# New queue orders for four engines of a transformer block on one Trainium2 core

## Chip, cores and metric

The kernel runs on one core of a Trainium2 chip. The metric is the time of one execution in microseconds (us); the median of several runs is given. The core has a matrix engine (TensorE, in the profile PE, with its weight loads as PEld), a vector engine (VectorE, DVE), an activation engine (ScalarE, ACT), a general engine (GpSimd, POOL) and a queue that only issues transfers here (SyncE, SP). Each engine works off its own queue of instructions strictly in order; what crosses engines is held by semaphores.

## What is computed

One block over 2048 rows of 448 values, in bf16: a layer norm, linear attention with 16 heads of 28 features and a softmax feature map, a residual, a second layer norm, a gated feed-forward of width 1792, and a second residual.

```python
qkv = norm(x) @ wqkv                        # q, k, v: 16 heads, 28 features each
pq, pk = q @ w_phi, k @ w_phi               # per head
phi_q = concat([softmax(pq), softmax(-pq)]) # over the features of a head
phi_k = concat([softmax(pk), softmax(-pk)])
kv = einsum("bhsf,bhsd->bhfd", phi_k, v);  z = phi_k.sum(over s)
o = (phi_q @ kv) / (phi_q @ z + 1e-6)
h = x + o @ wo
g, u = norm(h) @ w_gate, norm(h) @ w_up
out = h + (sigmoid(g) * u) @ w_down
```

## The kernel before

The rows lie in 16 tiles of 128, numbered 0 to 15; four tiles make a chunk of 512. A class Graph takes every step as a named operation with its reads and writes, and derives from the program's order who must wait for whom. The order in which an engine works off its steps is another thing: it is written out by hand in the table ORDER, one string of names per engine. A step that may run on more than one engine (given as a tuple of engines) runs on the one whose string has its name. So a change of the strings moves steps in a queue or between engines, and touches neither the work nor the dependences. No planner runs when the kernel is built.

The names, in the order of the work, with the number of the tile behind them and the line of the profile in brackets:

- Start: warm (L478) are matmuls on zeros; zero, bd0, v1ones, phipad, opad0, mask0 to mask2, ident0, ident, neghalf and wqpad fill constants. x1, x0, x2, ... load tiles of x (x2 loads tiles 2 and 3, and so on); ld_k, ld_v, ld_q, wphi load attention weights.
- Layer norm 1: bst and agg (L499, L500) are the statistics, ve1, pow1, nm1, nb1 (L507, L512, L510, L516) make the reciprocal deviation and the shift, xn (L525 on ScalarE, L528 on VectorE or GpSimd) the normalised tile. The rstd steps serve groups: tiles 0, 1, 2, 3, then 4-5, 6-7, 8-11, 12-15, named by the first. xT turns the tile over: tiles 0 to 3 by a matmul (L492) and a copy xTe (L485), the others by a transfer that SyncE issues (L538).
- Weights folded with w_phi: wT (L554), its copy wTe, w2m (L567), its copy w2e (both copies L485); w2m0, w2e0 for k, w2m1, w2e1 for q.
- Projections of k and v (L296): ppa, ppb and vva, vvb for tiles 0 to 3 in pairs, pva, pvb for one tile from 4 on. An "a" and a "b" step are the two halves of one accumulation on the array's two row halves, and b waits for a. Then v1 copies v out (L485), ek takes both exponentials (L614, L615), ss and rs the softmax sums and reciprocals (L618, L619), phi the product (L622), and kva, kvb (L296) add phi times v into two banks that kvzA to kvzD (L683, L687) copy out at the end; kvzones sets their ones. Three buffers hold phi, five each ek and v1.
- Attention per chunk and tile: pqa, pqb (L296) and eq (L652, L653) for q; num (L296), and behind it rsm, qq, b, c, den, rden on VectorE (L714 to L725), o (L729), oT (two by L492, the others by SyncE, L742), woa, wob (L296) and h (L748 on ScalarE, L751 on VectorE). num of all tiles from 2 on writes the same two banks, so it waits for the den before it.
- Layer norm 2: nm, sq, ve, pow2, hn (L754, L756, L759, L761, L765), hT (two by L492, the others by SyncE, L772).
- Feed-forward: ga, gb (L296) with gate and up, sig (L824), hh (L825), dn, dp, dm, dl (L296, L852) with w_down, fin (L859), out. ga0_1 is the second feature block of tiles 0 and 1; ga2, ga4, ga8 and ga12 are the later groups of tiles.

An evacuation may run on ScalarE or VectorE, xn on up to three engines, phi and o on GpSimd or VectorE:

```python
op(("act", "dve"), name, (lambda e: e.copy(dst, src), lambda e: e.tensor_copy(dst, src)), r=[rkey], w=[wkey])
op(("act", "dve", "pool"), "xn%d" % t, (fa, fd, fd), r=r + [("nb1", a)], w=[("xn", s)])
op(("pool", "dve"), "phi%d" % t, fphi, r=[("ek", s), ("rs", s)], w=[("phi", sp)])
```

## Time and profile before

| | |
|---|---|
| median of 3 runs | 205.54 us (205.32 to 205.71) |
| span of the profiled execution | 203.7 us, 5834 instructions |
| time of the profiled execution outside its span | not listed; the median of the runs is 1.8 us over the span |
| busy share of the span | PE 97%, PEld 55%, DVE 67%, ACT 48%, POOL 28% |
| TensorE clock granted | 1.00 of full speed in every stretch |

The span runs from the first to the last instruction of the program. Busy times are in us. The chain that ended last is followed back from the last instruction: at each step to what released it, or to the instruction before it on its engine. A line of a timeline has the start in us from the span's start, the time in us, the engine, the line of the kernel, the operation, what it writes and reads, how many were merged, and in brackets the idle time of the engine before it and who ended it. A tile view gives durations as least, median and most.

### The profile page before, as it was taken

To read this page: it belongs to the slowest core of one execution; us is meant where nothing else is said; L and a number is where in the kernel's file an instruction comes from. 1 tells how busy PE (TensorE), PEld (TensorE's weight loads), DVE (VectorE), ACT (ScalarE), POOL (GpSimd) and SP (SyncE) were. 2 spreads that over 40 slices of the span, in tenths; PEclk is the share of its full clock that TensorE was granted. 3 is DMA by queue.
4 is the path that set the end of the run, shared out by engine and by line. 5 is a ranking of instruction groups with operands and counts; after the bars stand their busy time and mean duration, and the time that the engine had idled before them with its cause. 6 is when DMAs were issued, how large, how long until landed. Compare 5 with 4: busy or idle time off the path is not lost.

```text
span 203.7 us, 5834 instructions
## 1 busy us (share of the span) xinstructions
PE 196.7 (97%) x2474; PEld 111.6 (55%) x2474; DVE 135.9 (67%) x340; ACT 97.4 (48%) x195; POOL 57.9 (28%) x98
## 2 busy tenths in 40 slices
...
GB/s 163 306 139 122 77 73 66 282 295 352 141 52 55 55 100 27 55 81 0 3 0 80 119 30 28 2 77 24 56 36 60 3 0 3 0 0 138 0 0 90
DMA packets 32866, 16.25 MB, mean 80 GB/s; under 512 B 25096, under 2 KB 31944, under 8 KB 32840
## 3 DMA queue, kind: packets, MB, share of 16 engines
...
q8 instruction: 19, 0.31, 0.7%
q10 hardware_dynamic: 504, 0.03, 0.2%
...
## 4 chain that ended last, share of the span: by engine, by line
PE 89%; DVE 4%; ACT 3%; DMA 1%; issue 1%; POOL 0%; DVEq 0%
PE psum L296 82%; PE psum L852 5%; DVE st L499 2%; DMA x_sb<-in_A_x_dram 1%; ACT eq L653 1%; ACT eq L652 1%; PE psum L567 1%; ACT junk L756 1%; ACT x_sb L748 1%; PE psum L492 1%; DVE kvz L683 1%; DVE mv L500 0%; DVE b_sb L717 0%; DVE c_sb L720 0%; POOL rst L512 0%
## 5 line engine op out<-in xcount | busy, mean ns | idle before, releaser
L296 PE MATMUL psum<-xnT,wg_sb 64*128 64x512 bf16 (+1 forms) x490 | 93.3, 333 | 0.4 <-ACT eq L653 0.2
L296 PE MATMUL psum<-xnT,wu_sb 64*128 64x512 bf16 (+1 forms) x490 | 93.0, 333 | 0.0
L824 ACT ACTIVATE sg_sb<-psum 128x512 bf16<-128x512 f32 (+1 forms) x70 | 35.0, 512 | 89.6 <-PE psum L296 89.0
L825 DVE SCALAR_TENSOR_TENSOR hhT<-sg_sb,psum 128x512 bf16<-128x512 bf16 (+1 forms) x70 | 39.0, 577 | 52.5 <-ACT sg_sb L824 52.1
L296 PEld LDWEIGHTS psum<-xnT,wg_sb 64*128 64x128 bf16 x490 | 44.3, 94 | 22.9 <-DVE hhT L825 4.8
L296 PEld LDWEIGHTS psum<-xnT,wu_sb 64*128 64x128 bf16 x490 | 44.3, 94 | 13.0
L296 PE MATMUL psum<-wd_sb,hhT 64*128 64x448 bf16 x336 | 36.9, 349 | 0.0
L296 PEld LDWEIGHTS psum<-wd_sb,hhT 64*128 64x128 bf16 x336 | 17.3, 94 | 14.8 <-DVE x_sb L751 0.6
L622 POOL TENSOR_TENSOR phi<-hhT,rs 128x896 bf16<-128x896 bf16 x14 | 24.1, 1738 | 0.9 <-PE psum L296 0.8
L296 PE MATMUL psum<-Wk,xnT 64*128 64x448 bf16 x112 | 22.3, 350 | 0.2
L296 PE MATMUL psum<-wv_sb,xnT 64*128 64x448 bf16 x112 | 22.4, 351 | 0.1
L759 POOL TENSOR_SCALAR ve<-ssq 128x1 f32<-128x1 f32 x16 | 3.1, 192 | 66.1 <-ACT junk L756 65.7
L618 DVE TENSOR_REDUCE ss<-hhT 128x32 f32<-128x896 bf16 x16 | 17.0, 1062 | 0.7 <-ACT hhT L615 0.7
L296 PE MATMUL psum<-xnT,Wq 64*120 64x512 bf16 x112 | 15.0, 385 | 0.1
L729 POOL TENSOR_TENSOR o_pad<-c_sb,rden 128x448 bf16<-128x448 bf16 x10 | 9.3, 936 | 15.6 <-DVE rden L725 13.4
L296 PE MATMUL psum<-wo_o,oT 64*128 64x448 bf16 x56 | 13.2, 350 | 0.0
L296 PE MATMUL psum<-wo_e,oT 64*128 64x448 bf16 x56 | 13.1, 349 | 0.0
L756 ACT ACTIVATE junk<-x_sb,nm 128x448 bf16<-128x448 bf16 x16 | 10.6, 661 | 1.9 <-DVE nm L754 1.8
L852 PE MATMUL psum<-wd_sb,hhT 128*128 128x448 bf16 (+2 forms) x70 | 11.1, 316 | 0.0
L859 DVE SCALAR_TENSOR_TENSOR x_sb<-psum,x_sb 128x448 bf16<-128x448 f32 (+2 forms) x17 | 9.4, 591 | 2.1 <-PE psum L852 1.6
L499 DVE BATCH_NORM_STATS2 st<-x_sb 128x6 f32<-128x448 bf16 x16 | 9.4, 611 | 1.9 <-DMA x_sb<-in_A_x_dram 1.9
L296 PEld LDWEIGHTS psum<-Wk,xnT 64*128 64x128 bf16 x112 | 7.6, 94 | 5.3 <-ACT hhT L615 0.7
...
## 6 DMA issues: line engine op xcount, KB each, us to landing
...
```

The lines of the kernel that those rows point to most:

```text
L296: p = e.matmul(o, lhsT=w, rhs=r, start=st, stop=sp, tile_position=(row, 0))
L492: p = e.transpose(ps[:, kt * P:(kt + 1) * P], src, ident[:])
L499: op("dve", "bst%d" % t, lambda e: e.bn_stats(st1[:, t, :], x_sb[:, t, :]), r=[("x", t)], w=[("st1", t)])
L618: op("dve", "ss%d" % t, lambda e: e.tensor_reduce(ss[:, s, :], eks, AX.X, ALU.add), r=[("ek", s)], w=[("ss", s)])
L622: return e.tensor_tensor(phi[:, sp, :, :, :].rearrange("p b a n -> p (b a) n")[:, :, 0:56].rearrange("p b (h d) -> p b h d", h=2), eks.rea ...
L729: return e.tensor_tensor(o_pad[:, t % NO, off:off + D].rearrange("p (h d) -> p h d", h=H), c_sb[:, t % NS, :, 0:DH], rden[:, t % NS, :][:, ...
L756: op("act", "sq%d" % t, lambda e: e.activation(junk[:, t % 2, :], h_sb[:, t, :], ACT.Square, bias=nm2[:, t:t + 1], accum_out=ssq2[:, t:t + ...
L759: op("pool", "ve%d" % t, lambda e: e.tensor_scalar(ve2[:, t:t + 1], ssq2[:, t:t + 1], 1.0 / D, EPS, op0=ALU.mult, op1=ALU.add), r=[("ssq2" ...
L824: op("act", "sig" + nm, lambda e: e.activation(sg_sb[:, k, 0:N], bk(bg)[:, 0:N], ACT.Tanh, scale=0.5), r=[B(bg)], w=[("sg", k)])
L825: op("dve", "hh" + nm, lambda e: e.scalar_tensor_tensor(out=hhT[(t0 // 4) % NHH][:, ff, ns], in0=sg_sb[:, k, 0:N], scalar=1.0, in1=bk(bu)[ ...
L852: p = e.matmul(bk(b)[:, lo:hi], lhsT=hb[:, ff, TS(t)], rhs=wd_sb[:, ff, lo:hi], start=ff == 0, stop=ff == FT - 1)
L859: op("dve", "fin%d%s" % (t, nm), lambda e: e.scalar_tensor_tensor(out=h_sb[:, t, lo:hi], in0=bk(b)[:, lo:hi], scalar=0.5, in1=h_sb[:, t, l ...
```

## The change

The strings of ScalarE, TensorE, VectorE and GpSimd are computed anew up to about the first groups of gate and up; behind them they are as they were, and SyncE's has the same names in the same order (its lines are only wrapped in another place). Some steps also change the engine:

- from ScalarE to VectorE: wTe0, wTe2, xT1e, kvzones; from ScalarE to GpSimd: xn4
- from VectorE to GpSimd: xn0, xn1, nm1_0, nm1_6, nm1_8, ve1_1, ve1_12, phi10, o8
- from GpSimd to VectorE: nm1_1, nm1_2, nm1_3, nm1_4, nm1_12, ve1_0, ve1_2, ve1_3, ve1_6, phi11, o2, o7

TensorE keeps all its steps. No operation, load, buffer or dependence is added or removed.

```diff
     "act": (
-        "wphi3 wphi2 wphi1 wphi0 wTe0 wTe1 xT1e xT0e wTe2 w2e0_0 w2e0_1 w2e0_2 w2e0_3 xn3 xn4 ek0 ek1 xn5 v1_0 v1_1 "
-        "xn6 ek2 v1_2 v1_3 ek3 w2e1_1 ek4 v1_4 ek5 v1_5 w2e1_0 v1_6 ek6 xn11 ek7 v1_7 xn12 ek8 xn13 ek9 w2e1_3 w2e1_2 "
-        "ek10 xn14 ek11 xn15 v1_11 ek12 eq0_0 ek13 v1_13 ek14 v1_14 ek15 kvzones v1_15 eq0_1 kvzB eq1_0 eq1_1 eq2_0 "
-        "oT0e eq2_1 h1 h0 sq1 sq0 eq3_0 eq3_1 sig0_1 sig0_0 sig0_3 sig0_2 sig0_5 sig0_4 sq2 sig0_7 sig0_6 sq3 sig0_9 "
-        "sig0_8 sq5 sig0_11 sig0_10 sig0_13 sig0_12 sig2_1 sig2_0 sq4 sig2_3 sig2_2 sq7 sq6 sig2_5 sig2_4 sig2_6 "
...
+        "wphi3 wphi1 wphi2 wphi0 wTe1 w2e0_0 w2e0_2 w2e0_1 w2e0_3 xT0e xn3 ek0 ek1 xn5 v1_1 v1_0 xn6 ek2 v1_2 v1_3 "
+        "ek3 w2e1_1 ek4 v1_4 w2e1_0 ek5 v1_5 ek6 v1_6 xn11 ek7 v1_7 xn12 ek8 xn13 ek9 w2e1_2 w2e1_3 ek10 xn14 xn15 "
+        "ek11 v1_11 ek12 eq0_0 ek13 v1_13 ek14 ek15 v1_14 v1_15 eq0_1 kvzB eq1_0 eq1_1 eq2_0 oT0e eq2_1 h1 h0 sq1 "
+        "sq0 eq3_0 eq3_1 sig0_1 sig0_0 sig0_3 sig0_2 sig0_5 sig0_4 sig0_7 sig0_6 sq3 sq2 sig0_9 sig0_8 sig0_11 "
+        "sig0_10 sig0_13 sig0_12 sig2_1 sig2_0 sq4 sq5 sig2_3 sig2_2 sq7 sq6 sig2_5 sig2_4 sig2_6 sig2_7 sig2_8 "
...
     "pe": (
-        "warm0 warm1 warm2 wT0 wT1 xT1 warm3 xT0 warm4 warm5 wT2 w2m0_0 wT3 warm6 w2m0_1 w2m0_2 warm7 w2m0_3 warm8 "
-        "ppa0 warm9 ppb0 vva0 xT3 xT2 vvb0 ppa2 ppb2 vva2 vvb2 w2m1_1 w2m1_0 kva0 pva4 kvb0 pvb4 pva5 kva1 pvb5 kvb1 "
-        "pva6 kva2 pvb6 pva7 w2m1_2 w2m1_3 pvb7 pva8 kvb2 kva3 pvb8 kvb3 pva9 kva4 pvb9 kvb4 pva10 kva5 pvb10 pva11 "
-        "kvb5 kva6 pvb11 pqa0_0 pva12 kvb6 kva7 pvb12 kvb7 pqb0_0 kva8 pva13 kvb8 kva9 pvb13 pva14 kvb9 kva10 pvb14 "
-        "kvb10 kva11 pva15 kvb11 pvb15 kva12 pqa0_1 kvb12 pqb0_1 kva13 pqa1_0 kvb13 kva14 pqb1_0 kvb14 kva15 kvb15 "
-        "pqa1_1 num0 num1 pqb1_1 pqa2_0 pqb2_0 num2 pqa2_1 oT0 pqb2_1 oT1 num3 woa0 wob0 num4 pqa3_0 pqb3_0 pqa3_1 "
-        "num5 pqb3_1 hT1 hT0 num6 ga0_1 ga0_0 gb0_1 gb0_0 woa2 num7 ga0_3 ga0_2 gb0_3 gb0_2 wob2 ga0_5 ga0_4 gb0_5 "
-        "gb0_4 num8 woa4 ga0_7 ga0_6 gb0_7 gb0_6 wob4 num9 ga0_9 ga0_8 gb0_9 gb0_8 woa6 ga0_11 ga0_10 gb0_11 gb0_10 "
-        "wob6 ga0_13 ga0_12 gb0_13 gb0_12 dn0_0 dn0_4 ga2_1 ga2_0 gb2_1 gb2_0 dn0_8 dn0_11 ga2_3 ga2_2 gb2_3 num10 "
...
+        "warm0 warm1 warm2 warm3 warm4 warm5 wT1 wT0 wT2 wT3 w2m0_0 xT1 w2m0_2 warm6 w2m0_1 w2m0_3 warm7 xT0 warm8 "
+        "warm9 ppa0 ppb0 xT2 vva0 xT3 vvb0 ppa2 ppb2 vva2 vvb2 w2m1_1 w2m1_0 pva4 kva0 pvb4 pva5 kvb0 pvb5 kva1 "
+        "pva6 kvb1 pvb6 kva2 pva7 w2m1_3 kvb2 pvb7 pva8 kva3 w2m1_2 pvb8 kvb3 pva9 kva4 pvb9 kvb4 pva10 kva5 pvb10 "
+        "kvb5 pva11 pqa0_0 kva6 pvb11 pva12 kvb6 kva7 pvb12 kvb7 pqb0_0 kva8 pva13 kvb8 pvb13 kva9 pva14 kvb9 "
+        "kva10 pvb14 kvb10 kva11 pva15 kvb11 pvb15 pqa0_1 kva12 pqb0_1 kvb12 kva13 pqa1_0 kvb13 kva14 kvb14 kva15 "
+        "kvb15 pqb1_0 pqa1_1 num0 num1 pqb1_1 pqa2_0 pqb2_0 num2 pqa2_1 oT0 pqb2_1 oT1 num3 woa0 wob0 num4 pqa3_0 "
+        "pqa3_1 pqb3_0 num5 pqb3_1 hT1 hT0 num6 ga0_1 ga0_0 gb0_1 gb0_0 woa2 num7 ga0_3 ga0_2 gb0_3 gb0_2 wob2 "
+        "ga0_5 ga0_4 gb0_5 num8 gb0_4 woa4 ga0_7 ga0_6 gb0_7 gb0_6 wob4 ga0_9 ga0_8 gb0_9 gb0_8 woa6 ga0_11 ga0_10 "
+        "gb0_11 gb0_10 num9 wob6 ga0_13 ga0_12 gb0_13 gb0_12 dn0_0 dn0_4 ga2_1 ga2_0 gb2_1 gb2_0 dn0_8 dn0_11 "
...
     "dve": (
-        "zero bd0 bst1 agg1 ve1_1 bst0 agg0 nm1_0 xn1 xn0 bst2 agg2 bst3 agg3 bst4 bst5 wTe3 agg4 agg5 bst6 bst11 "
-        "bst10 agg11 bst9 bst7 agg6 agg7 agg9 bst8 agg8 agg10 xT3e xT2e ss0 nm1_8 nm1_6 rs0 ss1 bst13 rs1 bst12 ss2 "
-        "bst14 rs2 agg14 xn8 ss3 agg13 agg12 rs3 xn9 bst15 ss4 agg15 xn10 ve1_12 ss5 rs4 ss6 rs5 ss7 rs6 v1_8 ss8 "
-        "v1_9 rs7 ss9 rs8 v1_10 ss10 rs9 rs10 ss11 v1_12 rs11 phi10 ss12 rs12 ss13 rs13 ss14 rs14 ss15 rs15 phi15 "
-        "kvzA kvzD kvzC rsm0 qq0 b0 rsm1 c0 qq1 den0 b1 rden0 c1 rsm2 den1 qq2 rden1 b2 c2 den2 oT1e rsm3 qq3 b3 c3 "
-        "den3 rden2 rden3 rsm4 nm1 qq4 b4 nm0 c4 den4 rden4 hn1 rsm5 qq5 b5 hn0 c5 hT1e den5 hT0e rden5 rsm6 qq6 b6 "
-        "c6 den6 hh0_1 hh0_0 rsm7 rden6 qq7 b7 c7 hh0_3 den7 hh0_2 h2 rden7 nm2 h3 hh0_5 rsm8 hh0_4 qq8 b8 c8 nm3 "
-        "den8 hh0_7 hh0_6 h5 h4 rsm9 hn3 hh0_9 hh0_8 rden8 nm5 qq9 hn2 nm4 hh0_11 hh0_10 h7 h6 o8 hh0_13 hh0_12 b9 c9 "
-        "den9 rden9 o9 hh2_1 hh2_0 hh2_3 rsm10 hh2_2 hn4 qq10 nm7 b10 nm6 c10 hn5 hh2_5 hh2_4 hn6 fin0 fin1 hn7 hh2_6 "
...
+        "bd0 zero bst0 bst1 agg0 agg1 nm1_1 ve1_0 bst3 bst2 wTe0 agg3 wTe2 agg2 ve1_2 nm1_3 ve1_3 nm1_2 wTe3 xT1e "
+        "bst6 bst7 bst5 bst4 agg5 agg6 agg4 agg7 bst10 nm1_4 bst8 xT2e ve1_6 bst9 xT3e agg10 bst11 agg9 agg8 agg11 "
+        "ss0 rs0 bst12 ss1 rs1 ss2 bst13 rs2 bst14 xn8 ss3 agg13 rs3 agg14 xn9 bst15 agg12 agg15 ss4 xn10 rs4 "
+        "nm1_12 ss5 ss6 rs5 rs6 v1_8 ss7 v1_9 rs7 ss8 v1_10 rs8 ss9 ss10 rs9 ss11 rs10 v1_12 rs11 ss12 rs12 phi11 "
+        "ss13 rs13 ss14 rs14 ss15 rs15 phi15 kvzones kvzD kvzC kvzA rsm0 qq0 rsm1 b0 qq1 c0 den0 b1 rden0 c1 rsm2 "
+        "den1 qq2 rden1 b2 c2 den2 oT1e rsm3 qq3 b3 c3 den3 rden3 rsm4 qq4 rden2 nm1 b4 nm0 c4 den4 o2 rsm5 qq5 b5 "
+        "hn1 hn0 c5 hT1e den5 hT0e rden4 rsm6 qq6 rden5 b6 c6 den6 hh0_1 hh0_0 rsm7 qq7 b7 c7 hh0_3 hh0_2 den7 h3 "
+        "rden6 h2 rden7 hh0_5 hh0_4 o7 rsm8 nm2 qq8 b8 hh0_7 nm3 hh0_6 h4 h5 hh0_9 hh0_8 hn3 c8 den8 hn2 hh0_11 "
+        "hh0_10 h6 h7 rsm9 hh0_13 nm4 qq9 hh0_12 rden8 b9 nm5 c9 den9 rden9 o9 hh2_1 hh2_0 hh2_3 rsm10 hh2_2 hn4 "
+        "qq10 nm7 b10 nm6 c10 hn5 hh2_5 hh2_4 hn6 fin0 fin1 hn7 hh2_6 hh2_7 den10 rden10 hh2_8 hh2_9 h8 h9 hh2_10 "
...
     "pool": (
-        "neghalf ident0 ident phipad wqpad mask0 nm1_1 pow1_1 ve1_0 pow1_0 nm1_2 mask1 ve1_2 ve1_3 pow1_3 nm1_3 "
-        "pow1_2 nb1_3 ve1_4 nm1_4 pow1_4 nb1_4 nb1_2 xn2 mask2 opad0 ve1_6 pow1_6 ve1_8 v1ones pow1_8 nb1_6 phi0 "
-        "nb1_8 xn7 phi1 phi2 phi3 nm1_12 pow1_12 nb1_12 phi4 phi5 phi6 phi7 phi8 phi9 phi11 phi12 phi13 phi14 o0 o1 "
-        "o2 o3 ve1 pow2_1 ve0 pow2_0 o5 o4 o6 o7 ve2 pow2_2 ve3 pow2_3 ve5 ve4 pow2_4 pow2_5 ve7 pow2_7 ve6 pow2_6 "
-        "ve8 ve9 o11 pow2_9 o12 pow2_8 ve10 pow2_10 ve11 pow2_11 ve12 pow2_12 ve14 pow2_14 ve15 ve13 pow2_15 pow2_13 "
+        "v1ones mask0 phipad ident0 ident neghalf wqpad ve1_1 pow1_1 mask1 xn1 nm1_0 pow1_0 xn0 pow1_2 pow1_3 "
+        "nb1_3 nb1_2 mask2 xn2 ve1_4 pow1_4 nb1_4 xn4 pow1_6 nm1_6 nb1_6 ve1_8 nm1_8 pow1_8 phi0 xn7 nb1_8 phi1 "
+        "phi2 phi3 ve1_12 pow1_12 nb1_12 phi4 phi5 phi6 phi7 phi8 phi9 phi10 opad0 phi12 phi13 phi14 o0 o1 o3 ve1 "
+        "ve0 pow2_1 pow2_0 o4 o5 o6 ve3 ve2 pow2_3 pow2_2 o8 ve5 ve4 pow2_4 pow2_5 ve7 pow2_7 ve6 pow2_6 ve8 ve9 "
+        "o11 pow2_9 o12 pow2_8 ve10 pow2_10 ve11 pow2_11 ve12 pow2_12 ve14 pow2_14 ve15 ve13 pow2_15 pow2_13 "
```

## The prediction

> **What bounds the kernel now.** I read the page first, then the table of busy time by stretch, then the chain that ended last, and then the timeline of each engine. An engine's n-th instruction is the n-th name of its queue, so every start and end below has a name.
>
> ```profile
> PE 196.7 (97%) x2474; PEld 111.6 (55%) x2474; DVE 135.9 (67%) x340; ACT 97.4 (48%) x195; POOL 57.9 (28%) x98
> ...
> PE 89%; DVE 4%; ACT 3%; DMA 1%; issue 1%; POOL 0%; DVEq 0%
> ```
>
> TensorE carries the chain, but the 97% is an average. By stretch (columns: stretch, length, then busy us of PE, PEld, DVE, ACT and POOL):
>
> ```profile
> 1.20:10.20 9.00, 8.18 (x84) 5.24 (x86) 6.78 (x20) 5.87 (x11) 5.26 (x18) 1.00 1.05 266
> ...
> 18.00:30.00 12.00, 12.00 (x195) 6.90 (x195) 11.34 (x25) 11.71 (x26) 11.65 (x10) 1.00 0.53 87
> 30.00:40.00 10.00, 10.00 (x192) 6.11 (x190) 9.78 (x16) 9.67 (x19) 9.15 (x7) 1.00 0.57 165
> ...
> 46.20:61.00 14.80, 13.06 (x208) 6.98 (x209) 13.08 (x44) 13.65 (x21) 5.27 (x9) 1.00 0.61 179
> ...
> 76.00:204.00 128.00, 125.36 (x1364) 67.72 (x1358) 68.75 (x163) 38.16 (x80) 10.30 (x25) 1.00 0.16 36
> ```
>
> From 18 to 40 us four engines are full at once; from 76 us TensorE runs alone, and there both orders are the same but for a few names. So the change can only move the moment at which TensorE gets into that last stretch.
>
> ```profile
> 2.87 0.64 DVE st L499
> ...
> 8.84 0.30 DVE WkT L485
> ...
> 9.59 0.54 ACT Wk L485
> ...
> 18.03 5.95 PE psum L296 x90
> ...
> 24.48 18.74 PE psum L296 x336
> ...
> 45.71 0.41 DVE kvz L683
> ...
> 75.42 51.27 PE psum L296 x684
> ```
>
> In the chain, the first projection ppa0 (10.18) hangs on wTe3, which VectorE does late, behind bst4 and bst5. From 18 us on TensorE hardly waits, until VectorE's kvz copies release num0 at 46.20.
>
> The page times a span of 203.7 us; the median of the runs is 205.54, so 1.8 us lie around the span. I move times within the span and add the shift to 205.54.
>
> **Start-up.** TensorE's and ScalarE's names are the same work in another order; the engine changes are what costs. VectorE now begins with bst0, which needs x0. The tile view of x_sb, kept to x0's issue at 1.25, gives 2.6 us to landing: 3.87, one microsecond after x1 (2.84), with which it began before. bst0 and bst1 (0.53 from start to start) and the two agg end at 5.28. GpSimd then has, in its queue's order, ve1_1 0.24, pow1_1 0.57, mask1 0.33, xn1 0.77, nm1_0 0.23, pow1_0 0.57, xn0 0.77; with 0.08 before each that reads the one before, xn0 ends at 8.83 (before: 6.25, on VectorE at 0.41 each). The transposition xT0 (0.40) and its copy xT0e on ScalarE (0.59) follow: ppa0 at 9.94. The old limit is gone: wTe0, wTe2, wTe3 on VectorE start at 6.50, 6.87 and 7.63, and w2e0_3 ends at 9.36. So ppa0 comes 0.24 earlier. xT2 and xT3 no longer stand together (0.1 saved), and xn4 goes from ScalarE to GpSimd, ahead of ek0. Then ek1 ends at 13.62 instead of 13.95, and pva4 starts near 17.6 instead of 18.21. xn4 ends at 13.45 instead of 12.21, which holds SyncE's xT4 and what stands behind it (xT5, x14, xT6); xT5 waits for xn5 until 14.3 anyway, and pva4 needs xT4 only at 17.6, while it lands by 17.2 even with the longest 3.7 us of the tile view of xn_pad.
>
> **18 to 46 us.** TensorE's lead of 0.5 is lost again if VectorE is late, and it is. VectorE until ss0: 12 bst x 0.53, 12 agg x 0.10, 3 wTe x 0.29, 3 xT copies x 0.34 and 8 small ones x 0.07 make 10.0; two waits for xT2 and xT3 make 0.47 more; from 3.90 this gives ss0 at 14.4, against 13.79. From ss0 to phi11, the step that VectorE takes over from GpSimd for phi10: 13 ss x 0.99, 13 rs x 0.26, 4 bst x 0.53, 4 agg x 0.09, 3 xn x 0.31, 4 v1 x 0.52, one nm1, 0.33 where rs stands right behind its ss, and 0.28 of waiting for ek11, which now stands behind xn15: 22.4. phi11 starts at 36.8 and ends at 38.2. kva11 needs it, and started at 38.26 before, behind GpSimd's phi11:
>
> ```profile
> 34.00 1.70 POOL L622 TENSOR_TENSOR phi<-hhT,rs 128x896 bf16<-128x896 bf16 x1 [0.39 <-PE psum L296]
> 36.11 7.06 POOL L622 TENSOR_TENSOR phi<-hhT,rs 128x896 bf16<-128x896 bf16 x4 [0.41 <-PE psum L296]
> ```
>
> So the lead shrinks to a few hundredths at kva11, whatever TensorE gained. pvb15, ek15 (41.18), ss15 1.10, rs15 0.39 and phi15 1.38 then follow each other as before: phi15 ends at 44.06 instead of 44.12. GpSimd is not late: phi9 in its new place starts near 33.5, opad0 (0.35) sits behind phi10, and phi14 ends before 43.1 instead of at 43.18. pqb1_0 now stands behind kvb15 and fills the 0.5 us in which TensorE waited for kvz, but it is missing ahead of kva15, where TensorE now waits about as long. kvzones (0.56 on ScalarE, three small copies) lies on VectorE between phi15 and kvzD, behind kvb15's wait, so it costs nothing; without that cover it costs up to 0.5. num0: 46.15, 0.05 earlier.
>
> **46 to 61 us.** ScalarE's eq steps set the pace, in the same order. Then o2 (0.62, read from VectorE's o8) moves into VectorE's queue ahead of rsm5, hn1 goes behind b5, and ve0 stands ahead of pow2_1. Summed along VectorE: den4 ends 0.16 earlier, o2 adds 0.54 net, hn1 and hn0 run together, and hT0e ends at 60.73 instead of 60.68. So +0.05, between -0.2 (if num4 and num5 come as early as den4 allows) and +0.3 (if pow2_1, now waiting for sq0, becomes the last).
>
> **61 to 79 us.** num9 leaves its place ahead of ga0_9, where hh0_7 is awaited anyway (70.73), and fills the 0.20 that TensorE waited at ga0_13: +0.03. The transposes get later. rden6 goes behind h3, so o6 ends at 67.98 instead of 65.13; o7 goes to VectorE behind hh0_4 and ends at 69.25 instead of 68.02, so oT7 is issued at 69.3, not 68.05. By the tile view of oT (2.4 to 3.1 us to landing) it lands between 71.7 and 72.4; woa6 wants it at 72.33. hn2 ends at 74.8 instead of 73.97, hT2 lands 2.4 to 4.2 us after 74.95 (tile view of xnT), and ga2_1 wants it at 78.5. o8 on GpSimd and rsm9, qq9 behind num9 stay ahead of num10 and woa8. I take +0.1 for both together, between 0 and 0.7.
>
> Sum: -0.05 + 0.05 + 0.03 + 0.1 = +0.13, so 205.7.
>
> **A rule against this change.** The xn steps move to the slower engine, and beside a busy VectorE. The trace has GpSimd's xn twice, both times with VectorE's statistics or sums beside it:
>
> ```profile
> L528 DVE TENSOR_SCALAR xn_pad<-x_sb,nm,rst x5: 375/406/414, 4.9 to 23.3; 128x512 bf16<-128x512 bf16 x5
> ...
> L528 POOL TENSOR_SCALAR xn_pad<-x_sb,nm,rst x2: 772/772/772, 11.6 to 17.4; 128x512 bf16<-128x512 bf16 x2
> ```
>
> They did not vary, so I take 0.77 and nothing on top. Yet the four phi that start at 36.11 take 7.06, which leaves 2.09 for the first against 1.70 for others, and VectorE's phi10 ran until 36.65. The Trainium skill, "SBUF — State Buffer", section "SBUF: two separate sides", says that VectorE and GpSimd share a port pair as an exclusive lock, which one of them holds for a whole instruction if VectorE's reads two SBUF tiles or is in a two-port mode. By the rows the sum stays at 205.7; by the rule, if xn1 and xn0 each met such an instruction, it would be near 206.5.
>
> **Rivals.** *Faster: the lead stays.* VectorE's waits for xT2, xT3 and ek11 (0.75 together in my sum) come from my own estimates of TensorE and ScalarE; without them phi11 and phi15 end up to 0.5 earlier, and the lead of 0.45 at pva9 reaches num0: 205.1, and 204.8 if hT0e gains its 0.2 too. Against it: VectorE is 9.78 of 10 us busy in 30 to 40 already. *Slower: GpSimd's start-up chain.* Seven steps now stand in line between agg1 and xT0. If xn1 and xn0 each lose what phi11 lost (2.09 - 1.70 = 0.39), or x0 lands later, ppa0, ek0, xT2e, ss0 and phi11 slide with it one for one: +0.8, 206.4. It decides from ppa0 later than about 10.3. *Slower too: the transposes.* the tile view of oT has issues of 1.19 to 1.97 us; with 1.97 for oT6, oT7 is issued at 69.95 and with 3.1 lands at 73.05, so woa6 waits 0.7: 206.3. It decides once oT7 lands after 72.33. *Not what it says:* names change beyond the first gate groups (sq5, o8, rden8), up to 82 us; if all early effects cancel that is all there is, which lies within the forecast.
>
> **How the numbers follow.** 0.2% is 0.41 us, about what a measurement of this kernel can tell from no change: 205.13 to 205.95. Forecast, early gains eaten by VectorE, 0.50, its own range 205.3 to 206.2; lead stays 0.22; GpSimd's chain 0.17; transposes 0.11. Of the forecast 0.34 lies within the bound, 0.03 below, 0.13 above. So faster 0.25, same 0.34, slower 0.41. The range takes the rivals' own values: 204.9 to 206.6.
>
> **What would show it.** First L296 matmul near 9.9, and GpSimd's first L528 at 6.5; pva4 near 17.6; TensorE idle just before kva11 near 38 us and before kva15 near 44, put down to VectorE's phi; num0 near 46.1; ga0_1 within 0.2 of 61.0. Wrong if ppa0 starts after 10.3, if TensorE reaches num0 before 45.8, or if woa6 or ga2_1 waits for a transpose by more than 0.3.

## The result, and the profile after

The changed kernel takes 206.81 us (median of 4 runs, 206.21 to 207.25) against 205.43 us for the kernel before on the same chip (4 runs, 205.27 to 205.71): ratio 1.0065, 95% interval 1.0045 to 1.0084. The ratios here and below are estimated from the runs and need not be the quotient of two medians. The forecast was 205.7 with a range from 204.9 to 206.6. The profiled execution of the changed kernel is the shortest of its runs, 206.21 us with a span of 204.5 us, so 1.7 us lie around the span. Its trace explains 0.8 us over the span of before (203.7); the 0.6 to 1.0 us more of the other three runs are in no trace. In some kernels below a part of the runs has a mean granted TensorE clock of 0.992 instead of 1.00 and takes about 2 us longer.

Line numbers after are higher by two: L296 is L298, L485 is L487, L499 is L501, L528 is L530, L622 is L624. First the two lines of the page after, then its busy time by stretch (stretch, length, busy us of PE, PEld, DVE, ACT, POOL).

```profile
PE 197.0 (96%) x2474; PEld 113.0 (55%) x2474; DVE 136.8 (67%) x349; ACT 94.7 (46%) x188; POOL 58.5 (29%) x96
...
PE 86%; DVE 7%; DMA 2%; ACT 2%; SPq 1%; issue 1%
```

```profile
1.20:10.20 9.00, 8.23 (x84) 5.47 (x84) 5.88 (x22) 3.99 (x7) 6.04 (x19) 1.00 1.01 264
18.00:30.00 12.00, 11.81 (x190) 6.78 (x188) 11.74 (x26) 11.25 (x25) 11.69 (x12) 1.00 0.45 96
30.00:40.00 10.00, 10.00 (x198) 6.09 (x194) 9.61 (x17) 9.97 (x20) 9.55 (x8) 1.00 0.52 140
46.20:61.00 14.80, 13.13 (x200) 6.96 (x196) 13.23 (x44) 13.61 (x21) 4.37 (x7) 1.00 0.71 201
```

In the first 9 us VectorE is busy 5.88 us instead of 6.78 and ScalarE 3.99 instead of 5.87: both wait more, and they lack that time later. The chain that ended last (start, time, what) shows on whom in the start-up:

```profile
2.68 4.34 DMA wk_sb<-in_A_wqkv_dram
7.06 0.62 PE psum L556 x8
8.03 1.84 ACT Wk L487 x4
9.86 0.50 ACT xnT L487
10.50 0.95 PE psum L298 x8
...
43.43 1.32 DVE phi L624
```

Before, the first projection ppa0 (10.18) hung on wTe3. Now it hangs on a row of ScalarE's evictions: the four w2e0 and, queued behind them, xT0e; ppa0 starts at 10.50. The row begins behind wT2, whose load landed at 7.01 (6.30 before). At the end of the stage TensorE now waits 0.31 us for phi15 ahead of kva15; before, it waited 0.49 us for kvz ahead of num0 instead.

Followed by names, TensorE is late by 0.32 us at ppa0, 0.13 at pva4, 0.40 at pva8, 0.70 at pva9, 0.73 at kva11, 0.69 at num0 (46.89 against 46.20), 0.72 at ga0_1, 0.73 at woa6, 0.82 at ga2_1 and 0.78 at its last step. So the loss is there before num0, and nothing is added or given back later but 0.1. The timeline of VectorE shows where it begins:

```profile
4.86 0.14 DVE L509 TENSOR_SCALAR ve<-mv 128x1 f32<-128x1 f32 x1
6.08 1.15 DVE L501 BATCH_NORM_STATS2 st<-x_sb 128x6 f32<-128x448 bf16 x2 [1.08 <-DMA x_sb<-in_A_x_dram]
7.16 0.37 DVE L487 COPY WkT<-psum 112x448 bf16<-112x448 bf16 x1
...
8.57 0.42 DVE L487 COPY xnT<-psum 128x512 bf16<-128x512 bf16 x1
```

VectorE has done everything for x0 and x1 at 5.0 and then waits 1.08 us for x2. In the kernel before xn1 and xn0 lay in that time:

```profile
4.86 0.41 DVE L528 TENSOR_SCALAR xn_pad<-x_sb,nm,rst 128x512 bf16<-128x512 bf16 x1
5.84 0.41 DVE L528 TENSOR_SCALAR xn_pad<-x_sb,nm,rst 128x512 bf16<-128x512 bf16 x1 [0.57 <-POOL rst L512]
```

The evictions it took over (wTe0, wTe2, xT1e) all come behind x2. ss0 starts at 14.95 instead of 13.79, and xn8 ends at 21.09 instead of 20.09. The way from there to TensorE is a transfer: SyncE issues xT8 at 21.11 (before 20.12), and it lands at 25.27 (before 23.04). pva8 reads it, and ScalarE's xn11, which overwrites the buffer that xT8 reads, waits 0.49 us for it; before, xn11 waited for nothing. First after, then before:

```profile
25.29 0.81 ACT L527 ACTIVATE xn_pad<-x_sb,nb,rst 128x512 bf16<-128x512 bf16 x1 [0.49 <-DMA xnT<-xn_pad]
```

```profile
24.55 0.84 ACT L525 ACTIVATE xn_pad<-x_sb,nb,rst 128x512 bf16<-128x512 bf16 x1
```

Behind xn11 stand ek7 and v1_7, and pva9 waits for v1_7 (ended at 27.39, before 26.69).

### The profile page after: what moved, and what is told of

The parts are those of the page before. It is cut to its first block, busy times and chain, and to the rows that moved or that the text cites. A ratio compares the mean times of both kernels' runs of the same rounds, so it can differ in the third digit from the quotient of the medians.

```text
span 204.5 us, 5837 instructions
## 1 busy us (share of the span) xinstructions
PE 197.0 (96%) x2474; PEld 113.0 (55%) x2474; DVE 136.8 (67%) x349; ACT 94.7 (46%) x188; POOL 58.5 (29%) x96
## 4 chain that ended last, share of the span: by engine, by line
PE 86%; DVE 7%; DMA 2%; ACT 2%; SPq 1%; issue 1%
PE psum L298 79%; PE psum L854 5%; DMA wk_sb<-in_A_wqkv_dram 2%; DVE b_sb L719 1%; ACT Wk L487 1%; DVE c_sb L722 1%; SPq L397 1%; PE psum L494 1%; DVE phi L624 1%; DVE hhT L827 1%; DVE ss L620 1%; DVE o_pad L731 1%; DVE rsm L716 0%; PE psum L569 0%; DVE qq L717 0%
## 5 line engine op out<-in xcount | busy, mean ns | idle before, releaser
L298 PE MATMUL psum<-xnT,wg_sb 64*128 64x512 bf16 (+1 forms) x490 | 93.5, 333 | 0.4 <-DVE rden L727 0.2
L298 PE MATMUL psum<-xnT,wu_sb 64*128 64x512 bf16 (+1 forms) x490 | 93.1, 333 | 0.0
L298 PEld LDWEIGHTS psum<-xnT,wg_sb 64*128 64x128 bf16 x490 | 44.2, 94 | 22.9 <-DVE hhT L827 5.0
L298 PEld LDWEIGHTS psum<-xnT,wu_sb 64*128 64x128 bf16 x490 | 44.2, 94 | 12.7
L298 PE MATMUL psum<-wd_sb,hhT 64*128 64x448 bf16 x336 | 36.9, 349 | 0.0
L298 PEld LDWEIGHTS psum<-wd_sb,hhT 64*128 64x128 bf16 x336 | 17.8, 94 | 14.4 <-DVE x_sb L753 0.6
L624 POOL TENSOR_TENSOR phi<-hhT,rs 128x896 bf16<-128x896 bf16 x14 | 23.8, 1728 | 0.5 <-PE psum L298 0.5
L298 PE MATMUL psum<-Wk,xnT 64*128 64x448 bf16 x112 | 22.7, 350 | 0.5 <-ACT xnT L487 0.2
L298 PE MATMUL psum<-wv_sb,xnT 64*128 64x448 bf16 x112 | 22.8, 351 | 0.1
L298 PE MATMUL psum<-xnT,Wq 64*120 64x512 bf16 x112 | 14.6, 383 | 0.1
L731 POOL TENSOR_TENSOR o_pad<-c_sb,rden 128x448 bf16<-128x448 bf16 x9 | 8.4, 937 | 21.0 <-DVE rden L727 20.8
L298 PE MATMUL psum<-wo_o,oT 64*128 64x448 bf16 x56 | 13.2, 350 | 0.0
L298 PE MATMUL psum<-wo_e,oT 64*128 64x448 bf16 x56 | 13.1, 348 | 0.0
L501 DVE BATCH_NORM_STATS2 st<-x_sb 128x6 f32<-128x448 bf16 x16 | 9.3, 608 | 3.0 <-DMA x_sb<-in_A_x_dram 3.0
L298 PEld LDWEIGHTS psum<-Wk,xnT 64*128 64x128 bf16 x112 | 7.5, 93 | 5.3 <-PE psum L298 1.0
```

The lines of the kernel that those rows point to most:

```text
L298: p = e.matmul(o, lhsT=w, rhs=r, start=st, stop=sp, tile_position=(row, 0))
L501: op("dve", "bst%d" % t, lambda e: e.bn_stats(st1[:, t, :], x_sb[:, t, :]), r=[("x", t)], w=[("st1", t)])
L624: return e.tensor_tensor(phi[:, sp, :, :, :].rearrange("p b a n -> p (b a) n")[:, :, 0:56].rearrange("p b (h d) -> p b h d", h=2), eks.rea ...
L731: return e.tensor_tensor(o_pad[:, t % NO, off:off + D].rearrange("p (h d) -> p h d", h=H), c_sb[:, t % NS, :, 0:DH], rden[:, t % NS, :][:, ...
```

## Experiments

Medians are given as measured; "full clock" leaves out the runs at 0.992, and the last group tells where these come from. The moments are from each kernel's one profiled execution, in us.

| kernel | median (full clock) | ss0 | num0 | oT7 lands | woa6 |
|---|---|---|---|---|---|
| before | 205.42 to 205.49 | 13.79 | 46.20 | 71.11 | 72.33 |
| after | 206.81 | 14.95 | 46.89 | 72.67 | 73.06 |
| e1_mid | 206.74 (206.62) | 15.26 | 47.24 | 73.06 | 73.43 |
| e2_start | 206.44 (206.40) | 15.02 | 46.99 | 72.71 | 73.12 |
| e3_both | 206.64 (206.54) | 15.17 | 46.99 | - | - |
| e4_before_dma | 205.41 | 13.73 | 46.12 | 71.58 | 72.24 |
| e5_warm | 206.58 (206.28) | 15.04 | 46.87 | 72.61 | 73.03 |
| e6_oldstart | 207.56 (206.89) | 13.80 | 46.13 | 73.28 | 73.32 |
| e7_newstart | 206.20 | 15.20 | 46.90 | 71.94 | 73.07 |
| e8_before_phi | 205.34 | 13.84 | 46.06 | 71.53 | 72.21 |
| e9_before_o | 206.95 | 13.85 | 46.31 | 74.07 | 74.12 |
| e10_oldstart_o | 205.83 (205.59) | 14.10 | 46.33 | - | - |
| e11_after_o | 206.50 (206.45) | 14.49 | 46.56 | 72.64 | 72.73 |
| e12_before_evict | 206.59 | 14.76 | 47.17 | 72.52 | 73.29 |
| e13_before_lull | 206.04 (205.64) | 13.86 | 46.31 | 71.38 | 72.64 |
| e14_nolull | 206.95 (206.59) | 13.77 | 46.21 | - | - |
| e15_start_act | 206.67 | 15.34 | 47.24 | 72.21 | 73.37 |
| e16_before_o7 | 205.91 | 13.79 | 46.11 | 71.47 | 72.86 |
| e17_old46 | 205.66 | 13.64 | 46.12 | 71.25 | 72.29 |
| e18_before_xn | 205.78 | 14.32 | 46.52 | 71.51 | 72.67 |

A dash stands where the profiled execution had the lower clock by then.

### First theories: TensorE's middle order, or the first loads

e1_mid puts five names between 18 and 29 us back:

```diff
-  act  ek4 v1_4 w2e1_0 ek5 v1_5 ek6 v1_6
+  act  ek4 v1_4 ek5 v1_5 w2e1_0 v1_6 ek6
-  pe   pva7 w2m1_3 kvb2 pvb7 pva8 kva3 w2m1_2 pvb8
+  pe   pva7 w2m1_2 w2m1_3 pvb7 pva8 kvb2 kva3 pvb8
```

> The changed kernel, with five names of the stage from 18 to 29 us put back: ScalarE's w2e1_0 behind v1_5 and v1_6 ahead of ek6; TensorE's w2m1_2 ahead of pvb7 and kvb2 behind pva8. Theory M (the 0.6 us between pva4 and kva11 are TensorE's own: pva7 and pva8 wait for v1_5 and v1_6, which ScalarE now does later, and w2m1_2 no longer fills that wait): pvb8 is back near 26.1, VectorE's waits at v1_8, v1_9 and ss11 (0.57 together) shrink, num0 comes at 46.3 to 46.4 instead of 46.89, and the time falls by about 0.5 us against the changed kernel (206.3). Theory S (the 0.6 are VectorE's, which starts its statistics of x2 0.7 us later because x2 lands later, so that ss0 is at 14.95 and phi11 ends at 38.93 whatever TensorE does): kva11 still at 38.9 to 39.0 with a TensorE wait in front of it, num0 at 46.8, time as the changed kernel (206.8).

Measured: 206.74 us, ratio 1.0072 (1.0042 to 1.0101). From pva8 to pvb8 the time fell from 1.28 to 1.00 us as theory M said, and it was lost again at pva9, which waited for ScalarE's v1_7 (27.76) and started at 27.86: there xn11 had waited for xT8 until 25.64. kva11 starts at 39.35. M falls. Of S only the lateness holds: phi11 ended at 39.28, but kva11 follows the last matmul of kvb10 (39.32) without a wait.

e2_start puts VectorE's first fills and ScalarE's loads back, e3_both both edits, e4_before_dma the new first loads into the kernel before:

```diff
-  act  wphi3 wphi1 wphi2 wphi0
+  act  wphi3 wphi2 wphi1 wphi0
-  dve  bd0 zero
+  dve  zero bd0
```

> The changed kernel with the order of its first fills and loads put back: zero ahead of bd0 on VectorE, and wphi3 wphi2 wphi1 wphi0 on ScalarE. Theory S: x2 lands near 5.3 instead of 6.06 and ld_k2 near 6.3 instead of 7.01, VectorE's ss0 comes at 14.3 to 14.4, phi11 ends near 38.4, and the time falls by 0.3 to 0.6 us against the changed kernel (206.2 to 206.5). Theory M: the landings come earlier, but pva7, pva8 and w2m1_2 stay where they are, pvb8 at 26.6, num0 at 46.8, the time within 0.1 us of the changed kernel (206.7 to 206.8). If x2 still lands near 6.06, its landing does not hang on the order of these loads.

> The changed kernel with both put back: the first fills and loads, and the five names between 18 and 29 us. Both theories: num0 near 46.2 and the time near the kernel before plus the 0.1 us of the later stages, 205.5 to 205.7. If the time stays above 206.2, a third part of the change carries the loss.

> The kernel before, with only the order of the first fills and loads of the changed one: bd0 ahead of zero, wphi3 wphi1 wphi2 wphi0. If this order makes x2 and ld_k2 land 0.7 us later, bst2 starts at 6.1 to 6.9 as before (VectorE had it behind xn0 until 6.17) and wTe2 near 8.2, so ppa0 moves by 0.3 to 0.7; VectorE has 0.0 to 0.2 of waiting in 12 to 14 us to give, so the time rises by 0.2 to 0.5 (205.7 to 206.0). If the landing is only scatter between executions: x2 near 5.3 and the time within 0.1 of the kernel before.

Measured: 206.44 (ratio 1.0052, 1.0033 to 1.0070), 206.64 (1.0071, 1.0046 to 1.0097) and 205.41 us (0.9998, 0.9983 to 1.0013). x2 landed at 6.13 in e2_start with the old order of loads, at 5.51 in e4_before_dma with the new one, and over all traces anywhere from 5.3 to 6.4: its landing does not hang on this order, and the kernel before does not mind it. The time of e2_start lies in S's range, but neither of S's signs came (x2 at 6.13, ss0 at 15.02). In e3_both x2 was early (5.59) and ss0 late all the same (15.17), since wTe0 had to wait for wT0 until 7.32. The timelines of TensorE, first e3_both, then the kernel before, show why:

```profile
1.24 5.41 PE L478 MATMUL psum<-zero 128*128 128x512 bf16 x22 [1.24 <-DVE zero L399]
6.44 1.30 PE L554 MATMUL psum<-ident,wk_sb 112*112 112x112 bf16 x16
```

```profile
1.24 3.56 PE L478 MATMUL psum<-zero 128*128 128x512 bf16 x11 [1.24 <-DVE zero L399]
4.81 0.62 PE L554 MATMUL psum<-ident,wk_sb 112*112 112x112 bf16 x8
```

The new order does 11 more warm-up matmuls (warm3, warm4, warm5) before the first useful step, and in this execution TensorE was still at half pace: its warm-up matmuls of 128 columns followed each other at 0.107 us up to 6.3 and at 0.055 us from 8.5 on, the smaller ones of wT at 0.09 us until 7.1 and at 0.05 us after. Both S and M are too small; the third part that e3_both's expectation allowed for exists.

### The start-up

e5_warm puts the 11 warm-up matmuls behind wT0:

```diff
-  pe   warm2 warm3 warm4 warm5 wT1 wT0 wT2
+  pe   warm2 wT1 wT0 warm3 warm4 warm5 wT2
```

> The changed kernel with TensorE's warm3, warm4 and warm5 (11 small matmuls) behind wT1 and wT0 instead of ahead of them. Theory W (the transpositions wT1 and wT0 wait for matmuls of no use, 0.6 us where TensorE's clock is up by then and 1.2 us where it is not; wTe0 on VectorE, wTe1 and all evictions behind them are late by that): wT0 ends near 5.6 to 5.9 instead of 6.56 to 7.40, wTe0 starts near 6.7 to 7.2, ppa0 at 10.2 to 10.5, ss0 at 14.6 to 14.9, the time falls by 0.2 to 0.5 us against the changed kernel (206.3 to 206.6), and its highest run comes down from 207.3 to 208.4 to below 207. Theory V (VectorE's queue is simply longer: bst0, bst1, bst3, bst2 ahead of wTe0, three evictions and xT1e ahead of the statistics): ppa0 and ss0 within 0.1 of the changed kernel's, time 206.7 to 206.8.

Measured: 206.58 us, ratio 1.0074 (1.0044 to 1.0103); its five runs at full clock 205.52 to 206.58. wT0 ended at 6.07, 0.5 earlier, and nothing followed from it: x2 landed at 6.15 and bst3 and bst2 stand ahead of wTe0 on VectorE, which started it at 7.24. ppa0 10.59, ss0 15.04. In this trace V holds, not W, though the median lies in W's range.

e6_oldstart and e7_newstart cut the orders once per engine and exchange the halves: TensorE behind pva7, ScalarE behind v1_4, GpSimd behind nb1_12, VectorE behind ve1_12 (old) or nm1_12 (new).

```diff
   e6_oldstart:  heads of before + tails of after
-  dve  bd0 zero bst0 bst1 ... rs4 nm1_12 | ss5 ss6 rs5 rs6
+  dve  zero bd0 bst1 agg1 ... xn10 ve1_12 | rs4 ss5 ss6 rs5 rs6
   e7_newstart:  heads of after + tails of before
-  dve  zero bd0 bst1 agg1 ... xn10 ve1_12 | ss5 rs4 ss6 rs5
+  dve  bd0 zero bst0 bst1 ... rs4 nm1_12 | ss5 ss6 rs5
```

> The changed kernel with the start-up of the kernel before on all four engines: TensorE's queue through pva7, ScalarE's through v1_4, VectorE's through ve1_12, GpSimd's through nb1_12 (opad0 early with it); from there the changed orders. Theory S2 (all of the loss is made in the start-up, and VectorE carries it to kva11 since it has no idle time to lose it in): ss0 at 13.8, phi11 on VectorE ends at 37.0 to 37.8, kva11 at 38.0 to 38.4, num0 at 45.8 to 46.3, time 205.0 to 205.6. Theory R (the later orders, from pva8 on, lose 0.3 us or more by themselves): num0 at 46.5 or later, time above 205.9.

> The other half: the kernel before with the start-up of the changed one on the four engines, cut at the same places (opad0 behind phi14). Theory S2: ss0 near 15, GpSimd's phi1 at 19.2 and phi11 there ends near 39.3 (38.21 before), num0 at 46.9 to 47.3, time 206.5 to 207.0. Theory R: num0 at 46.3, time 205.5 to 205.7.

Measured: e7_newstart 206.20 us, ratio 1.0040 (1.0028 to 1.0052): the new start-up alone costs 0.74 us, and num0 comes at 46.90 (S2's time, 206.5 to 207.0, was too high). e6_oldstart 207.56 us, ratio 1.0111 (1.0081 to 1.0142): num0 is back at 46.13, kva11 at 38.43, and yet it is slower than the changed kernel. So S2 is right up to num0 and wrong for the whole: R has its loss too, but at a place that neither expectation named, woa6 at 73.32 instead of 72.33. Of the 1.45 us by which this trace is late at its last step 1.0 is there at woa6; 0.5 comes at woa10, which waits for oT10 (landed at 113.74).

e12_before_evict and e18_before_xn do one half of the start-up's engine changes each in the kernel before, and e15_start_act takes the evictions back in e7_newstart:

```diff
   e12_before_evict
-  act  wTe0 wTe1 xT1e xT0e wTe2 w2e0_0
+  act  wTe1 xT0e w2e0_0
-  dve  xn1 xn0 bst2 agg2 bst3 agg3
+  dve  xn1 wTe0 xn0 xT1e bst2 agg2 wTe2 bst3 agg3
   e18_before_xn
-  dve  nm1_0 xn1 xn0 bst2
+  dve  nm1_0 bst2
-  pool pow1_1 ve1_0 pow1_0 nm1_2
+  pool pow1_1 xn1 ve1_0 pow1_0 xn0 nm1_2
-  pe   xT1 warm3 xT0 warm4 warm5 wT2 w2m0_0
+  pe   xT1 warm3 warm4 warm5 wT2 xT0 w2m0_0
-  act  wTe1 xT1e xT0e wTe2
+  act  wTe1 xT1e wTe2 xT0e
   e15_start_act
-  act  wTe1 w2e0_0 w2e0_2 w2e0_1 w2e0_3 xT0e xn3
+  act  wTe1 wTe0 wTe2 w2e0_0 w2e0_2 w2e0_1 w2e0_3 xT0e xT1e xn3
-  dve  wTe0 wTe2 xT1e (each in its place)
```

> The kernel before with wTe0, wTe2 and xT1e moved from ScalarE to VectorE as in the changed kernel, xn1 and xn0 left on VectorE. Theory D (VectorE's work behind the landing of x2 decides; the evictions add 0.9 us, of which its idle time before xn0 takes 0.4): ss0 comes at 14.2 to 14.5 instead of 13.79, phi1 and phi11 on GpSimd later by 0.4 to 0.7, time 205.7 to 206.1. Theory X (the loss is GpSimd's xn1 and xn0 and the late xT0, not the evictions): ss0 within 0.2 of 13.8, time 205.4 to 205.6.

> The kernel before with xn1 and xn0 alone moved from VectorE to GpSimd, each behind its pow; xT0 on TensorE behind wT2 and xT0e on ScalarE behind wTe2, so that neither is waited for in its old place; all evictions stay on ScalarE. Theory D (only work that VectorE gets behind x2's landing counts): VectorE has 0.8 us less, but it only waits longer for xT3 and xT2 (13.1 and 13.3), ss0 stays at 13.7 to 13.9, time 205.3 to 205.6. Theory X (GpSimd's slower xn costs): xT0e late, ppa0 at 10.5 or later, time 205.8 or more.

> The kernel with the changed start-up and the old rest (206.20), with wTe0, wTe2 and xT1e taken back to ScalarE (wTe0 behind wTe1, wTe2 behind it, xT1e behind xT0e). Theory D (the evictions on VectorE carry the start-up's loss): VectorE has 1.1 us less before ss0, which comes at 13.9 to 14.4 instead of 15.0 to 15.2, num0 at 46.2 to 46.5, time 205.4 to 205.8. Theory X (GpSimd's xn1 and xn0 and the late xT0): ppa0 stays at 10.5 or later, ek0 holds ss0, time 206.0 or more. ScalarE has 1.3 us more work between wTe1 and xT0e, of which 1.0 falls into its idle time.

Measured: the evictions alone 206.59 us, ratio 1.0044 (1.0031 to 1.0058), ss0 at 14.76 and num0 at 47.17: D, and more than D's ranges (14.2 to 14.5, 205.7 to 206.1); 0.3 us of this trace comes only at woa10. VectorE's timeline in e12_before_evict has them as

```profile
5.71 0.39 DVE L485 COPY WkT<-psum 112x448 bf16<-112x448 bf16 x1 [0.45 <-PE psum L554]
...
6.34 0.42 DVE L485 COPY xnT<-psum 128x512 bf16<-128x512 bf16 x1
...
7.62 0.39 DVE L485 COPY WkT<-psum 112x448 bf16<-112x448 bf16 x1
...
9.72 0.37 DVE L485 COPY WkT<-psum 112x448 bf16<-112x448 bf16 x1
```

The first fills idle time; the others push every statistic and wTe3, which started at 8.75 before, now starts at 9.72, so that ppa0 comes at 11.14. The move of xn1 and xn0 alone: 205.78 us against 205.46, ratio 1.0012 with an interval of 0.9993 to 1.0031, which can't be told from none; its trace has ppa0 at 10.70 and num0 0.32 late, in an execution in which x2 landed at 6.44 and wT0 ended at 6.12. VectorE waited for x2 and began bst2 at 6.47 instead of 6.17, and xT8 landed only at 25.10. D's bounds are missed, by 0.2 us in the time and by 0.4 in ss0 (14.32); X's ppa0 is met and its time nearly, but xn1 and xn0 took 0.77 us each, like GpSimd's xn steps in the trace of before. Whether their move costs anything stays open. e15_start_act: 206.67 us, ratio 1.0064 (1.0049 to 1.0079): the time and the ppa0 (10.88) that X gave, but not by X's way. VectorE reached bst6 at 7.92, a microsecond sooner, and then waited 1.33 us for xT2, which TensorE does behind ppb0; ppa0 itself waited until 10.88 for xT1e, which the edit had put behind xT0e. So the start-up has several limits close together (VectorE's queue, ScalarE's row of evictions, TensorE's order), and taking one away lets the next one bind. That xT0e stands behind the four w2e0 is one of them in every version with the new start-up.

### The transposes

e9_before_o takes one piece of the later order into the kernel before, e16_before_o7 only its second half; e10_oldstart_o and e11_after_o take it out of e6_oldstart and of the changed kernel:

```diff
   e9_before_o
-  dve  rsm7 rden6 qq7 b7 c7 hh0_3 den7 hh0_2 h2 rden7 nm2 h3 hh0_5 rsm8 hh0_4 qq8
+  dve  rsm7 qq7 b7 c7 hh0_3 den7 hh0_2 h3 rden6 h2 rden7 nm2 hh0_5 hh0_4 o7 rsm8 qq8
-  pool o5 o4 o6 o7 ve2
+  pool o5 o4 o6 ve2
   e16_before_o7
-  dve  hh0_5 rsm8 hh0_4 qq8
+  dve  hh0_5 hh0_4 o7 rsm8 qq8
   e10_oldstart_o, e11_after_o
-  dve  rsm7 qq7 ... h3 rden6 h2 rden7 hh0_5 hh0_4 o7 rsm8
+  dve  rsm7 rden6 qq7 ... h3 h2 rden7 hh0_5 hh0_4 rsm8
-  pool o4 o5 o6 ve3
+  pool o4 o5 o6 o7 ve3
```

> The kernel before with one piece of the later order: rden6 behind h3, o7 on VectorE behind hh0_4. Theory T (the transposes: o6 comes late, oT6's issue takes 1.2 to 2.2 us, oT7 is issued behind it and lands at 72.6 to 73.3, while TensorE, on time, wants woa6 at 72.33): o6 ends near 68.0, oT7 lands at 72.2 to 73.3, woa6 at 72.4 to 73.3, time 205.6 to 206.4, and its runs spread by up to 1 us. Theory S2 (only the start-up loses): 205.4 within 0.1.

> The changed kernel with the start-up of the kernel before, and now also rden6 back behind rsm7 and o7 back on GpSimd. Theory T: oT7 lands near 71.1, woa6 at 72.2 to 72.4, time 205.2 to 205.5, against 207.56 with the start-up alone put back. If something else in the later order loses, it stays above 206.

> The changed kernel with rden6 and o7 put back, its own start-up kept. Both losses stand one behind the other and the first hides the second: num0 stays at 46.9, woa6 at 73.0, so the fastest runs stay at 206.0 to 206.2; the slower ones, in which oT7 landed later than 73, go, and the median comes to 206.0 to 206.4 like that of the kernel with the new start-up alone (206.20). If start-up and transposes were additive, the time would fall to 205.7 or below.

> The kernel before with o7 alone moved from GpSimd to VectorE behind hh0_4; rden6 stays behind rsm7. If rden6 (the late o6 and oT6) is what delays oT7: oT6 is issued at 65.9, oT7 near 68.6 and lands at 71.6 to 72.2, woa6 at 72.3 to 72.4, time 205.4 to 205.6. If o7's engine is: oT7 lands after 72.5 and the time is 205.8 or more.

Measured: e9_before_o 206.95 us, 1.5 over the kernel before, ratio 1.0062 (1.0041 to 1.0084): T in kind, but beyond its range, and with runs only 0.4 apart. Its chain and, below, its list of waits between 61 and 80 us:

```profile
70.55 3.52 DMA oT<-o_pad
74.07 0.05 issue
74.12 3.02 PE psum L296 x41
```

```profile
PE psum L296 <- DMA oT<-o_pad: 0.9, 1, 0.9
```

rden6 at 66.87 instead of 63.92 makes o6 end at 68.13; SyncE is at oT6's issue from 68.16 to 70.51 (2.35), though o7 was ready at 69.17; oT7 then lands at 74.07, and woa6 wants it near 73.2. In the trace of after the same issue took 1.19, and oT7 was issued as soon as o7 was done. In e6_oldstart the same wait stands for the weight loads, while the waits of the matmuls name VectorE, whose hh0_8 ended 0.02 us later than oT7 landed (73.28); woa6 reads oT7 and not hh0_8:

```profile
PEld psum L296 <- DMA oT<-o_pad: 1.2, 1, 1.2
PE psum L296 <- DVE hhT L825: 0.9, 1, 0.9
```

e16_before_o7, 205.91 us, ratio 1.0022 (1.0013 to 1.0031), parts the two: with rden6 early oT7 lands at 71.47 in spite of o7 on VectorE, and its 0.5 us come from ga0_9, late by 0.53 because hh0_7 stands behind o7 (the changed kernel pushes c8 and den8 behind hh0_7 and is spared that). So of e9's 1.5 us about 1.0 is the transposes' own, made by rden6 and oT6's long issue together; the rest is hh0_7. An estimate from these rows: with an issue of 1.19 us oT7 would have been issued at 69.35 instead of 70.55 and landed near 72.9, ahead of woa6. Why the issue takes 1.19 us in one trace and 2.35 in another no run shows.

e10_oldstart_o comes to 205.83 (205.59 at full clock), ratio 1.0035 (1.0008 to 1.0063): without both parts the time is within 0.2 us of the kernel before, as long as the clock stays up. e11_after_o has 206.50 (206.45), ratio 1.0061 (1.0036 to 1.0086), its runs at full clock 205.87 to 206.87: the start-up's loss alone, as e7_newstart has it. The two are not additive: woa6 waits for the later of TensorE and oT7, 0.7 late the one and 1.0 late the other.

### phi10 and phi11

e8_before_phi exchanges them in the kernel before:

```diff
-  dve  rs11 phi10 ss12 rs12 ss13
+  dve  rs11 ss12 rs12 phi11 ss13
-  pool phi9 phi11 phi12
+  pool phi9 phi10 phi12
```

> The kernel before with one pair exchanged as in the changed kernel: phi10 on GpSimd behind phi9, phi11 on VectorE behind rs12. If GpSimd's phi11 (ends at 38.21) is what takes the lead of 0.45 us away that TensorE has at pva9, then phi11 on VectorE ends near 37.7 to 38.0, kva11 starts at 37.7 to 38.0, num0 comes at 45.8 to 46.0, and the time is 205.1 to 205.3. If VectorE is late either way, as in the prediction's sum: 205.5 within 0.1.

Measured: 205.34 us, ratio 0.9996 (0.9986 to 1.0005); phi11 ends at 38.17 instead of 38.21, kva11 starts at 38.22. The exchange is worth nothing either way, as the prediction's sum had it. No kernel of this study beats the one before.

### The lower clock

Of the runs of all kernels with the new order from 46 to 61 us or a part of it (e13_before_lull, e14_nolull) 27 of 91 had the lower clock, of those with the old order there none of 85, and of the kernel before 1 of 125. The windows of e10_oldstart_o's profiled execution (stretch, length, busy us of the five engines, then the granted clock) show where:

```profile
61.00:62.00 1.00, 0.83 (x14) 0.82 (x16) 0.96 (x4) 0.27 (x1) 0.93 (x2) 0.88 0.02 2
62.00:63.00 1.00, 1.00 (x14) 0.84 (x12) 0.93 (x3) 0.00 (x0) 0.90 (x2) 0.50 0.07 16
...
65.00:66.00 1.00, 1.00 (x30) 0.92 (x28) 0.43 (x3) 0.00 (x0) 0.00 (x0) 0.91 0.59 118
```

Half the clock from 61.76 to 65.18 (0.24 and 0.18 us of the outer windows at half), 3.4 us, and as long in the traces of e3_both and e14_nolull.

```diff
   e13_before_lull
-  dve  den4 rden4 hn1 rsm5 qq5 b5 hn0 c5
+  dve  den4 rden4 rsm5 qq5 b5 hn1 hn0 c5
-  pe   pqa3_0 pqb3_0 pqa3_1 num5
+  pe   pqa3_0 pqa3_1 pqb3_0 num5
   e14_nolull (on e10_oldstart_o)
-  dve  den4 o2 rsm5 qq5 b5 hn1 hn0 c5
+  dve  den4 o2 hn1 rsm5 qq5 b5 hn0 c5
-  pe   pqa3_0 pqa3_1 pqb3_0 num5
+  pe   pqa3_0 pqb3_0 pqa3_1 num5
   e17_old46 (on e10_oldstart_o)
   VectorE, GpSimd (o2, pow2_1) and pqb3_0 as in before from den3 to den6
```

> The kernel before with two swaps of the later order: hn1 behind b5 (so hn1 and hn0 run together), and pqa3_1 ahead of pqb3_0. TensorE then has nothing to do from the end of pqb3_1 (58.3 to 58.9) to hT1, about 1 us, and as before 0.7 us ahead of num6. Theory L (this lull lets the clock drop): some of the runs, 1 in 10 to 1 in 2, have a mean granted clock of 0.992 and are 2 us longer; the others 205.3 to 205.6. Theory N (the drop comes from elsewhere, for example from TensorE's unbroken work before num0): all runs at 1.0, time 205.3 to 205.6.

> The changed kernel with the old start-up and the old o chain (205.83), and now also hn1 back ahead of rsm5 and pqb3_0 ahead of pqa3_1. Theory L: no run at 0.992, the median comes to 205.3 to 205.6. Theory N: a third of the runs at 0.992 as without this.

> The changed kernel with the old start-up and the old o chain (205.83), and now the whole old order from 46 to 61 us: rden2 and rden4 back, hn1 ahead of rsm5, o2 on GpSimd, pqb3_0 ahead of pqa3_1. What is left of the change is the order from pva8 to num0 and the names beyond 61 us. Theory L (the lull drops the clock): no run at 0.992, time 205.3 to 205.6, the drop's share gone. Theory N (the drop comes from TensorE's unbroken work before num0): a third of the runs at 0.992 as before.

Measured: e13_before_lull 5 of 12 runs at 0.992 (ratio over all runs 1.0042, 1.0015 to 1.0069; the others 205.47 to 206.18); e17_old46 none of 12 and 205.66 us, ratio 1.0013 (1.0001 to 1.0025). e14_nolull still 2 of 6: o2 (0.62 us) stayed ahead of hn1, and the hole moved from before hT1 to before hT0 (ratio 1.0069, 1.0044 to 1.0093). In the traces the longest time without a matmul between 58 and 61 us is 0.88 to 0.97 us in every kernel of the first group (0.89 in the changed kernel, which had no such run in four) and 0.59 to 0.61 in the others, while TensorE's busy time there is the same (1.15 us of 58.50 to 61.00 both before and after). L is shown as to the place and the two swaps; that the single hole and not something else about them decides was not tried. All four runs of the changed kernel had the full clock, so this is no part of the measured 0.65%.

## Why the prediction was wrong, point by point

**VectorE until ss0: the size of the wait.** The work was sized right (10.0 us forecast, 10.1 measured between 3.38 and 14.95). The waiting was not: 0.47 us forecast, 1.4 measured, 1.08 of it at 5.00; that VectorE began 0.5 us sooner than forecast (x0 landed at 3.36, not 3.87) went into this wait. The sum added VectorE's work as if all of it could begin at 3.90. In the queue's order xn1 and xn0 had stood in a time in which nothing else is there to do, so taking them away gave nothing that could be measured, and the evictions came behind x2, where all of it counts. This is the first step that failed: ss0 14.95 instead of 14.4, and in eight traces with the new start-up 14.5 to 15.3.

**ppa0 at 9.94: measured 10.50.** GpSimd's chain was right and even quicker (first L530 at 6.02 instead of 6.5, xn0 done at 8.61 instead of 8.83; the terms listed there, with the two gaps of 0.08, make 8.92). "The transposition xT0 and its copy follow" was wrong: xT0 stands behind w2m0_3 and warm7 and ran at 9.31, and xT0e behind w2e0_3 at 9.74. The wTe started at 7.16, 7.53 and 8.28, not at 6.50, 6.87 and 7.63. The forecast's own mark for a miss, ppa0 later than 10.3, was passed.

**From VectorE to TensorE: phi11 and xT8.** phi11 began at 37.90, not 36.8: 0.55 from ss0, 0.55 on the way. xn8 took 0.72 instead of 0.31, and v1_8, v1_9 and ss11 waited 0.57 where 0.28 were allowed for. phi11 took 1.03 instead of 1.38 and ended at 38.93. kva11 started at 38.99, but not because it waited for phi11: the last matmul of kvb10 had started at 38.95.

TensorE was 0.70 us late already at pva9, and from pva9 to kva11 it takes 11.4 to 11.6 us in all twenty traces. What made it late there is the second step that failed, a term that the sum put at nothing: xT8's landing. The forecast followed SyncE's transfers only up to xT6. Without its wait for xT8, 0.49 us, xn11 would have been 0.25 us late; with it, it was 0.74. In all eight traces with the new start-up pva9 starts 2.2 us behind xT8's landing; in the others, but for e18_before_xn, xT8 lands 3.6 to 4.1 us ahead of pva9. xT8 was late by 1.0 us through VectorE's xn8 and by 1.2 more on its way (4.15 us from issue to landing instead of 2.92; 4.0 to 4.2 in all eight); why it takes longer no run shows. No kernel was run in which xT8 alone is early, so how far phi11 would have held kva11 by itself stays open; its own 0.57 us of waits were for TensorE and ScalarE.

TensorE's wait ahead of kva15 is there as forecast, 0.31 us, 0.7 late. pva4 at 18.34 was to be 17.6.

**num0.** 46.15 forecast, 46.89 measured. With the old start-up the changed order gave 46.13 and 46.12 (e6_oldstart, e17_old46): the amount for 18 to 46 us was right, the start it was given was not, and nor was the path: in e6_oldstart kva11 starts at 38.43, 0.25 us behind phi11's end. Of the 1.4 us between the medians the start-up is 0.74 (e7_newstart), and the trace of the changed kernel shows 0.8. The rest stays open; e11_after_o, without the later transposes, has 206.45 at full clock instead of 206.81, but its runs overlap with those of the changed kernel.

**46 to 61 us.** +0.05 forecast; 14.84 us from num0 to ga0_1 against 14.81: right, though the moved hn1 and pqa3_1 let the clock drop in other runs (above), which no step had. "hn1 and hn0 run together" was put down as free.

**61 to 79 us.** +0.13 forecast, +0.10 measured at ga2_1, right by luck: oT7 landed at 72.67, later than the forecast's 71.7 to 72.4 and later than woa6's 72.33, and only TensorE's own lateness hid it. By itself it costs 1.0 (e6_oldstart), a little over the 0.7 that the rival had: the forecast should not have taken +0.1 of 0 to 0.7 when oT6's issue can take over 2 us (2.11 in e6_oldstart, 2.35 in e9_before_o; the rival had 1.97, and why it varies no run shows).

**Rivals.** The transposes' mechanism was right and was given 0.11; that it costs time is shown by e9_before_o, e10_oldstart_o and e16_before_o7. GpSimd's chain named the right threshold and nearly the right time (206.4), but for a cause that did not occur: neither xn1 nor xn0 lost anything. "The lead stays" was out of reach. The forecast also missed that two losses standing one behind the other would leave no way for one to be saved without the other.

**The rule on the shared port.** For xn1 and xn0 the rows decided, and nothing on top was right (tile view of after):

```profile
L530 POOL TENSOR_SCALAR xn_pad<-x_sb,nm,rst x5: 766/771/773, 6.0 to 18.3; 128x512 bf16<-128x512 bf16 x5
L530 DVE TENSOR_SCALAR xn_pad<-x_sb,nm,rst x3: 378/405/717, 20.4 to 24.4; 128x512 bf16<-128x512 bf16 x3
```

The 717 is VectorE's xn8, at 20.37, while GpSimd's phi1 runs until 20.94. In all eight traces with the new start-up xn8 takes 0.70 to 0.86 us and ends 0.15 us behind phi1; in the twelve others, where it starts 0.2 us or less before phi1 ends, 0.38. The Trainium skill, "SBUF — State Buffer", section "SBUF: two separate sides", describes a port pair that VectorE and GpSimd share as a lock; the trace agrees there. The forecast looked for it on GpSimd's side only; it was VectorE that waited, 0.34 us at xn8, on the way to xT8 and phi11.
